# One core, attention and two mixtures of experts: a third expert taken in pairs of quarters, the last row tiles in ascending order, one group of relus behind a minimum

## The chip, the cores and the metric

The kernel runs on one core of a Trainium2 chip. A time is the device time in microseconds (us) of one execution. Five engines work side by side, each through its own list of instructions in order: TensorE (PE; its weight loads are shown as PEld), VectorE (DVE), ScalarE (ACT), GpSimd (POOL) and SyncE (SP), which issues most DMAs. They wait for one another by semaphores.

## The reference, cut to what matters

```python
def _attn_ref(q, k, v, w1, b1, w2):                  # 2 x 8 heads, 576 positions, 64 per head
    scores = scale * np.matmul(q, k.transpose(0, 1, 3, 2))
    x = (log1p(|i - j|) / log1p(max(i, 1)))[..., None]
    bias = np.maximum(x @ w1 + b1, 0.0) @ w2          # 32 hidden, 8 heads
    scores = scores + bias.transpose(2, 0, 1)[None]
    attn = softmax(scores)
    return np.matmul(attn, v)

def _moe_ref(x, w_gate, w1, w2, capacity):            # 1152 tokens, 8 experts, at most 288 each
    expert_idx = np.argmax(x @ w_gate, axis=1)
    ...
    h = np.maximum(np.einsum('ecd,edf->ecf', disp, w1), 0.0)
    y = np.einsum('ecf,efd->ecd', h, w2)              # 512 -> 1024 -> 512
    out[i] = gate_w[i] * y[expert_idx[i], pos[i]]     # a token over capacity stays zero

def _moe2_ref(x, w_in, w_out, alpha):                 # 512 -> 2048 -> 512, dense
    h = x @ w_in
    return (np.maximum(h, 0.0) + alpha * np.minimum(h, 0.0)) @ w_out
```

The dense layer's weights come in 64 bits and are turned into 32 bits on the chip. The matmuls of the experts and of the dense layer take each operand as two parts, a rounded high one and the rest (names that end in h and l), and add three products.

## The kernel before, in words

The program has five stages.

- Head: tables of relus make the position bias. `bias_h` computes four relu tiles of a block of 16 query rows (`h`, most on DVE at L183), `bias_mm` multiplies them (L192), `bias_out` scales the result on ACT (L200) and writes it to a scratch tensor `bd`, from where `load_bias` and `load_bias4` read it back as `bias`.
- Course: units of attention in slots. In a slot PE computes the scores of one unit, DVE adds the bias and takes the row minimum of the negated scores (`low`, L266), ACT takes the exponential (`expo`, L273), and PE turns the result of an earlier unit and multiplies it by the values. The first slots also carry what is left of the bias blocks: `tiles(1)` issues the four relus of one block, `blocks(2)` the matmuls of two. The order of PE, ACT and DVE in this stage is the order of the code.
- The first expert (`job`): 288 rows, eight steps; a step has 12 matmuls of `layer1` (L690) and 12 of `layer2` (L705). Quarters of the weights are split by `raw_split` into high and low parts, on ACT (L602) and DVE (L603).
- The second and the third expert, beside each other (`two_groups`). The second runs as `job` does. The third has at most 32 rows and goes along as a `rider`: its steps are called from inside the second expert's eight, at the numbers in the table `RT` (step 2f stands after `layer1` of f, 2f+1 after `layer2` of f-1). A rider transposes its rows, then takes four quarters of the weights: `partial` (four matmuls, side by side in four groups of 32 columns of the array), a copy on ACT (L803), `hidden` (fold, two matmuls, a relu on ACT), and later `layer2`; `load2` fetches the second weights into the room of the first. `ahead` converts the first weights of the dense layer in steps 3, 5 and 7.
- The dense layer (`ffn`): 608 rows in five tiles of 128 (the last has 96), 16 steps of 24 matmuls of `layer1` (L941) and 15 of `layer2` (L953). At its end each row tile gets the last two steps' six matmuls, is scaled by the gate on ACT (L979) or DVE (L981), and POOL scatters it to `out` (L982).

In the last two stages the code is not the order: a scheduler with a model of the costs places the instructions of every engine, and they then run in that order. It also keeps two engines from one tile, so that a matmul into a tile of two banks waits until the scale of the other half has been read. `facc` is such a tile: row tiles 0 and 1 share one, 2 and 3 another, and row tile 4 has `facc4` to itself.

## Time and profile before

| what | value |
|---|---|
| median of 3 runs | 359.77 us (359.17 to 360.88) |
| the profiled execution | 359.0 us, span 357.3 us |
| head and course | about 0 to 171 us of the span |
| second expert with the rider | 203 to 239 us |
| dense layer, to its last matmul | 239 to 350 us |
| last scatters and the end | 350 to 357 us |

The span runs from the first to the last instruction. The profile gives the busy time of each engine, the instructions in order of time with the idle time ahead of each and what ended it, the waits summed by pair, and the DMAs with the time from issue to landing. A 32-bit matmul stands in it as two records, so that four of them are "x8".

### The profile page before, as it was taken

How to read it: one execution, taken by the hardware profiler on the slowest of the kernel's cores; microseconds unless marked ns; L12 is line 12 of the kernel's file. 1: busy time of each engine (PE TensorE's matmuls, PEld its weight loads, DVE VectorE, ACT ScalarE, POOL GpSimd, SP SyncE). 2: the span in 40 equal slices, each digit the busy share in tenths (PEclk: the TensorE clock that was granted, in tenths of full speed). 3: DMA queues.
4: the chain of work that ended last, by engine and by line, in shares of the span. 5: the costliest groups of instructions: out<-in, count | busy, mean ns of one | idle time of the engine just before them, and what ended most of it. 6: DMA issues, size and time to landing. Idle time of an engine off the chain costs nothing. (4 is left out here: it accounts for less than half of the span.)

```text
span 357.3 us, 8970 instructions
## 1 busy us (share of the span) xinstructions
PE 339.5 (95%) x3372; PEld 273.2 (76%) x3373; DVE 278.7 (78%) x674; ACT 236.4 (66%) x585; POOL 58.8 (16%) x90
## 2 busy tenths in 40 slices
PE   4898999999999999999999999999999999999991
PEld 2334566677899788888899997799988988987880
DVE  4999989977788867876798795369999999988430
ACT  6959899987667675766774473357776656656430
POOL 2055333300000010462262100100000000000023
PEclk9999999999999999999999999999999999999997
DMA  7788969898999853948736996743546645530003
GB/s 301 223 257 273 333 244 354 313 285 313 339 411 337 276 206 108 332 154 258 222 71 189 361 288 187 246 150 125 178 119 189 190 152 178 175 120 3 0 29 118
DMA packets 42048, 76.90 MB, mean 215 GB/s; under 512 B 5159, under 2 KB 19623, under 8 KB 41996
## 3 DMA queue, kind: packets, MB, share of 16 engines
q1 hardware_dynamic: 40812, 73.76, 63.0%
q0 software_dynamic: 1184, 2.48, 1.9%
q8 instruction: 28, 0.46, 0.6%
q14 instruction: 24, 0.20, 0.2%
HBM read 57.53 MB, written 20.09 MB: 217 GB/s over the span
## 5 line engine op out<-in xcount | busy, mean ns | idle before, releaser
L273 ACT ACTIVATE p<-p,mn 128x576 f32<-128x576 f32 x72 | 55.6, 779 | 11.4 <-DVE mn L266 11.2
L259 PE MATMUL sps<-kqv 64*128 64x288 f32 x256 | 61.3, 427 | 0.3 <-DVE mn L266 0.2
L266 DVE CUSTOM_DVE_ANT_0 p<-sps,bias 128x576 f32<-128x576 f32 x72 | 52.4, 751 | 6.2 <-PE sps L252 3.6
L305 PE MATMUL t<-ident,p 64*128 64x64 f32 x640 | 52.6, 227 | 0.6 <-DVE PT L282 0.2
L183 DVE TENSOR_SCALAR h<-c 128x512 f32<-128x512 f32 (+17 forms) x121 | 49.5, 474 | 0.5 <-PE bps L192 0.4
L305 PEld LDWEIGHTS t<-ident,p 64*128 64x128 f32 x640 | 45.3, 139 | 6.0 <-ACT st L200 2.6
L280 ACT COPY PT<-t 128x320 f32<-128x320 f32 (+1 forms) x85 | 30.0, 404 | 24.7 <-PE sps L259 18.6
L259 PEld LDWEIGHTS sps<-kqv 64*128 64x128 f32 x256 | 37.2, 187 | 8.0 <-issue 4.1
L192 PE MATMUL bps<-h,c 128*32 128x512 f32 (+17 forms) x352 | 34.4, 489 | 8.0 <-DVE h L183 5.3
L323 PE MATMUL av<-PT,kqv 128*64 128x128 f32 x512 | 35.3, 279 | 0.8 <-ACT PT L280 0.3
L323 PEld LDWEIGHTS av<-PT,kqv 128*64 128x64 f32 x512 | 27.5, 137 | 8.6 <-ACT PT L280 4.1
L860 ACT ACTIVATE cv<-d 128x512 f32<-128x512 f32 x32 | 21.6, 676 | 14.8 <-DMA d<-in_win 5.5
L200 ACT ACTIVATE st<-bps,c 128x527 f32<-128x527 f32 (+35 forms) x72 | 30.6, 506 | 0.2 <-PE bps L192 0.2
L953 PE MATMUL facc<-w2h,hl 128*128 128x512 f32 (+1 forms) x75 | 29.9, 399 | 0.2 <-DVE hl L603 0.2
L953 PE MATMUL facc<-w2h,hh 128*128 128x512 f32 (+1 forms) x75 | 29.7, 396 | 0.0
L953 PE MATMUL facc<-w2l,hh 128*128 128x512 f32 (+1 forms) x75 | 29.6, 395 | 0.0
L192 PEld LDWEIGHTS bps<-h,c 128*32 128x32 f32 x352 | 10.6, 113 | 23.8 <-issue 7.4
L179 POOL TENSOR_SCALAR h<-c 128x448 f32<-128x448 f32 (+11 forms) x12 | 21.6, 1798 | 36.2 <-PE bps L192 19.5
L941 PE MATMUL fg<-yh,w1l 128*128 128x304 f32 x120 | 26.6, 303 | 0.0
L941 PE MATMUL fg<-yl,w1h 128*128 128x304 f32 x120 | 26.5, 302 | 0.0
L941 PE MATMUL fg<-yh,w1h 128*128 128x304 f32 x120 | 26.5, 302 | 0.0
L282 DVE COPY PT<-t 128x320 f32<-128x320 f32 (+1 forms) x43 | 18.8, 461 | 9.0 <-PE t L305 8.0
(232 smaller groups left out, 691.2 us busy)
## 6 DMA issues: line engine op xcount, KB each, us to landing
bias<-bd SPq DMA_DIRECT2D x23, 576.0 KB, 6.8
bd<-st SPq DMA_DIRECT2D x36, 295.5 KB, 6.7
raw<-in_ew SPq DMA_DIRECT2D x20, 512.0 KB, 6.5
d<-in_win SPq DMA_DIRECT2D x16, 512.0 KB, 3.8
d<-in_wout SPq DMA_DIRECT2D x16, 512.0 KB, 3.9
kqv<-in_kqva SPq DMA_DIRECT2D x6, 736.0 KB, 7.0
kqv<-in_kqvb SPq DMA_DIRECT2D x6, 672.0 KB, 9.3
xd<-zr SPq DMA_DIRECT2D x4, 722.8 KB, 8.6
```

The source lines that it names most:

```text
L179: G.tensor_scalar(h, tab[:, :n], psi[:, i:i + 1], 0.0, ALU.add, ALU.max)
L183: V.tensor_scalar(h, tab[:, :n], psi[:, i:i + 1], 0.0, ALU.add, ALU.max)
L192: T.matmul(ps[32 * c:32 * c + 32, n0:n1], w2n, hs[c][:, n0:n1], start=True, stop=True)
L200: A.activation(st[:, o:o + src.shape[1]], src, AF.Copy, scale=rr[:, t:t + 1])
L259: return [lambda n=n: T.matmul(ps[:, n, :288], q[u.ul][p], k[p, 288 * n:288 * n + 288], start=True, stop=True) for n in range(2)]
L266: V.tensor_tensor_reduce(out.rearrange("p (a b) -> p a b", a=2), ps[:, :, :288], bias.rearrange("p (a b) -> p a b", a=2), -0.125, 3.0e38, ...
L273: A.activation(out, out, AF.Exp, bias=mn, scale=-1.0, accum_out=acc)
L280: A.copy(o, i)
L305: return [lambda i=i, x=x: T.transpose(src[:, i], x[p], ident[p, p]) for i, x in enumerate(rows)], out
L323: T.matmul(o[p, c], u.v[:, j, p], rhs(h, j), start=j == 0, stop=False, skip_group_check=True)
L941: T.matmul(ps, w[:, 128 * k:128 * k + 128], x[:, k, s], start=k + i == 0, stop=k + i == 5)
L953: T.matmul(acc[i][:m], h[:, r:r + m], w, start=f == 0 and j == 0, stop=f == NF - 1 and j == 2)
```

## The change

Three edits. The rider takes two quarters in a call: `partial` puts two quarters into one tile of accumulators and copies 512 columns at once, `hidden` folds four pieces and takes one relu, `layer2` runs two quarters; the calls come at other steps, and so does `load2`. The last row tiles go in the order 0, 1, 2, 3, 4 in the code, 0 and 2 on DVE, 1 and 3 on ACT, and 4 in two halves, one on each. In slot 1 of the course the relus of one block are issued after the slot's minimum.

```diff
--- before.py
+++ after.py
@@ -33,7 +33,7 @@
 BIG = float(1 << 20)
 PRE0 = 10
 NB = 2
-RT = (0, 1, 2, 3, 4, 5, 6, 7, 9, 11, 12)
+RT = (4, 5, 7, 8, 10, 12, 14)
 Q3 = 1
 PRE = 4
 
@@ -794,29 +794,30 @@
                     T.transpose(ps[:, k], xr[:, 128 * k:128 * k + 128], ident[:n, :n])
                 V.tensor_copy(x, ps)
 
-            def partial(q):
-                w = S[q]
-                ps = ps1(pt, "part")[:, 0:256]
-                for k in range(4):
-                    T.matmul(ps[n * k:n * k + n], x[:, k], w[k], start=True, stop=True, skip_group_check=True)
-                R.p = cell()[:, 0:256]
+            def partial(*qs):
+                ps = ps1(pt, "part")
+                for q in qs:
+                    for k in range(4):
+                        T.matmul(ps[n * k:n * k + n, 256 * (q % 2):256 * (q % 2) + 256], x[:, k], S[q][k], start=True, stop=True,
+                                 skip_group_check=True)
+                R.p = cell()
                 A.copy(R.p, ps)
 
-            def hidden(q):
-                ps = ps1(pt, "hT")[:, 0:2 * n]
-                for j in range(2):
+            def hidden(*qs):
+                ps = ps1(pt, "hT")[:, 0:4 * n]
+                for j in range(4):
                     T.matmul(ps[:, n * j:n * j + n], R.p[:, 128 * j:128 * j + 128], fold[:, 2 * n:3 * n], start=True, stop=True)
-                A.activation(R.h[:, 2 * n * q:2 * n * q + 2 * n], ps, AF.Relu)
-
-            def layer2(q):
-                if q == 0:
+                A.activation(R.h[:, 2 * n * qs[0]:2 * n * qs[0] + 4 * n], ps, AF.Relu)
+
+            def layer2(*qs):
+                if 0 in qs:
                     R.acc = ps1(pt, "racc")[:, 0:256]
-                w = S[q]
-                for j in range(2):
-                    for d in range(2):
-                        o = n * (2 * j + d)
-                        T.matmul(R.acc[o:o + n], R.h[:, n * (2 * q + j):][:, 0:n], w[j][:, 256 * d:256 * d + 256],
-                                 start=q == 0, stop=q == 3, skip_group_check=True)
+                for q in qs:
+                    for j in range(2):
+                        for d in range(2):
+                            o = n * (2 * j + d)
+                            T.matmul(R.acc[o:o + n], R.h[:, n * (2 * q + j):][:, 0:n], S[q][j][:, 256 * d:256 * d + 256],
+                                     start=q == 0, stop=q == 3, skip_group_check=True)
 
             def finish():
                 y = cell()[:, 0:256]
@@ -831,10 +832,9 @@
                 V.tensor_tensor(yl, ps, yh.bitcast(F32), ALU.subtract)
 
             return begin, [(i, lambda f=f, q=q: f(*q)) for i, f, *q in (
-                (RT[0], transpose), (RT[1], partial, 0), (RT[1], load2, 0),
-                (RT[2], hidden, 0), (RT[2], partial, 1), (RT[2], load2, 1), (RT[3], hidden, 1), (RT[3], partial, 2), (RT[3], load2, 2),
-                (RT[4], hidden, 2), (RT[4], partial, 3), (RT[4], load2, 3), (RT[5], hidden, 3), (RT[6], layer2, 0),
-                (RT[7], layer2, 1), (RT[8], layer2, 2), (RT[9], layer2, 3), (RT[10], finish))]
+                (RT[0], transpose), (RT[1], partial, 0, 1), (RT[1], load2, 0), (RT[1], load2, 1),
+                (RT[2], hidden, 0, 1), (RT[2], partial, 2, 3), (RT[2], load2, 2), (RT[2], load2, 3), (RT[3], hidden, 2, 3),
+                (RT[4], layer2, 0, 1), (RT[5], layer2, 2, 3), (RT[6], finish))]
 
         def to_dense(acc, yo, n):
             for d in range(2):
@@ -968,13 +968,13 @@
                     prev = h
 
             ys = [z.bitcast(F32).rearrange("p (i n) -> p i n", i=2) for z in M.d]
-            for i in [i for i in (0, 2, 1, 3, 4) if i < len(rows)]:
+            for i in range(len(rows)):
                 r, m = rows[i]
                 layer2(i, NF - 2, *prev)
                 layer2(i, NF - 1, *h)
                 gt, ti = gts[i]
                 y = ys[i // 2][:, i % 2]
-                c = 0 if i in (2, 3) else DM
+                c = DM // 2 if i == 4 else DM if i % 2 else 0
                 if c > 0:
                     A.activation(y[:m, 0:c], acc[i][:m, 0:c], AF.Copy, scale=gt[:m, 0:1])
                 if c < DM:
@@ -1123,8 +1123,6 @@
                                   "places", "gates r2", "s0", "r3", "s1", "r4 s2", "s3", "s4 second", "", "halves", ""):
                             late.append([dict(first=first_weights, second=second, halves=first_halves).get(x) or st[x]
                                          for x in z.split()])
-                if i == 1:
-                    tiles(1)
                 turns(t, u)
                 expo(u)
                 b = blocks(2)
@@ -1138,7 +1136,7 @@
                     tiles(1)
                 if w:
                     b()
-                if nh < NT and i != 1:
+                if nh < NT:
                     tiles(1)
                 if u.short:
                     mix(scores(u.short, 0))
```

What moves on the engines. First, DVE in slot 1; `h` are relu tiles, `p,mn<-sps,bias` is the minimum of slot 1:

```order
 L183 TENSOR_SCALAR h<-c_81 128x448 x3
 L183 TENSOR_SCALAR h<-c_81 128x432 x4
+L266 ISA p_417,mn<-sps,bias_277 128x576
+L266 ISA mn 128x1
 L183 TENSOR_SCALAR h<-c_81 128x416 x3
-L266 ISA p_425,mn<-sps,bias_277 128x576
-L266 ISA mn 128x1
 L183 TENSOR_SCALAR h<-c_81 128x400 x4
```

The minimum moves ahead of three relus of one block.

Second, PE beside the second expert's step 4, from a fold of the rider on (`hT`; `part` is `partial`, `g` and `acc` are the second expert's own). Before:

```order
L808 MATMUL hT<-fold,cell 128x32 x2
L690 MATMUL g_3852<-xh,w1h 128x288
L690 MATMUL g_3852<-xl,w1h 128x288 x2
L801 MATMUL part<-raw_3393,m 32x256 x4
L690 MATMUL g_3852<-xl,w1h 128x288 x2
L690 MATMUL g_3852<-xh,w1l 128x288 x2
L808 MATMUL hT<-fold,cell 128x32 x2
L801 MATMUL part<-xj,m 32x256 x4
L690 MATMUL g_3852<-xh,w1l 128x288 x2
L705 MATMUL acc<-hh,w2h 128x288 x2
L808 MATMUL hT<-fold,cell 128x32 x2
L705 MATMUL acc<-hh,w2h 128x288 x2
```

And now:

```order
L809 MATMUL hT<-fold,cell 128x32 x4
L801 MATMUL part<-raw_3393,m 32x256 x4
L690 MATMUL g_3827<-xl,w1h 128x288 x2
L690 MATMUL g_3827<-xh,w1l 128x288
L801 MATMUL part<-xj,m 32x256 x2
L690 MATMUL g_3827<-xh,w1l 128x288 x2
L801 MATMUL part<-xj,m 32x256 x2
L690 MATMUL g_3827<-xh,w1l 128x288
L705 MATMUL acc<-hh,w2h 128x288 x4
L705 MATMUL acc<-hh,w2l 128x288
L809 MATMUL hT<-fold,cell 128x32 x4
L705 MATMUL acc<-hh,w2l 128x288 x3
```

The fold has four matmuls instead of two, and the last quarter's `partial` (`part<-xj`) stands in two pieces of two with the second expert's matmuls between them, where it stood in one. In the same stage, DVE behind the split of the first quarter (`w1l_...<-raw` is the split of the second quarter's first weights, `cv`, `cw` and `ah` belong to `ahead`). Before:

```order
L694 SCALAR_TENSOR_TENSOR hl_3662<-g1_3648,hh_3661 128x288 [waits Activation_49]
L862 TENSOR_SCALAR ah1_3437<-cv_3794 128x512 [waits Activation_49]
L863 SCALAR_TENSOR_TENSOR ah1_3437<-cv_3794,ah1_3437 128x512 [waits DVE_49]
L603 TENSOR_TENSOR w1l_3673<-raw_3630,w1h_3672 128x1024 [waits DMAHW7_49,Activation_49]
L694 SCALAR_TENSOR_TENSOR hl_3702<-g1_3688,hh_3701 128x288 [waits Activation_49]
L864 SCALAR_TENSOR_TENSOR ah1_3437<-d2_3119,ah1_3437 128x512 [waits DMAHW6_49,DVE_49]
```

And now:

```order
L694 SCALAR_TENSOR_TENSOR hl_3662<-g1_3648,hh_3661 128x288 [waits Activation_49]
L862 TENSOR_SCALAR cw_3702<-cv_3703 128x512
L862 TENSOR_SCALAR ah1_3437<-cv_3749 128x512 [waits Activation_49]
L863 SCALAR_TENSOR_TENSOR cw_3702<-cv_3703,cw_3702 128x512 [waits DVE_49]
L603 TENSOR_TENSOR w1l_3666<-raw_3630,w1h_3665 128x1024 [waits DMAHW7_49,Activation_49]
L694 SCALAR_TENSOR_TENSOR hl_3687<-g1_3673,hh_3686 128x288 [waits Activation_49]
```

A further conversion (`cw_3702<-cv_3703`, L862) stands ahead of the split of `w1l`, and its second step (L863) has taken the place of the other conversion's.

Third, the end of the dense layer on PE, the last 12 matmuls. Before (`facc_4028` holds row tiles 2 and 3):

```order
L953 MATMUL facc_4028<-w2h_4881,hh_5037 128x512 [waits DVE_49]
L953 MATMUL facc_4028<-w2l_4882,hh_5037 128x512
L953 MATMUL facc_4028<-w2h_4881,hl_5038 128x512
L953 MATMUL facc_4028<-w2h_4881,hh_5090 128x512
L953 MATMUL facc_4028<-w2l_4882,hh_5090 128x512
L953 MATMUL facc_4028<-w2h_4881,hl_5091 128x512
L953 MATMUL facc4_4029<-w2h_4881,hh_5037 96x512
L953 MATMUL facc4_4029<-w2l_4882,hh_5037 96x512
L953 MATMUL facc4_4029<-w2h_4881,hl_5038 96x512
L953 MATMUL facc4_4029<-w2h_4881,hh_5090 96x512
L953 MATMUL facc4_4029<-w2l_4882,hh_5090 96x512
L953 MATMUL facc4_4029<-w2h_4881,hl_5091 96x512
```

And now (`facc_4018` holds row tiles 2 and 3):

```order
L953 MATMUL facc4_4019<-w2h_4871,hh_5027 96x512
L953 MATMUL facc4_4019<-w2l_4872,hh_5027 96x512
L953 MATMUL facc4_4019<-w2h_4871,hl_5028 96x512
L953 MATMUL facc4_4019<-w2h_4871,hh_5080 96x512
L953 MATMUL facc4_4019<-w2l_4872,hh_5080 96x512
L953 MATMUL facc_4018<-w2h_4871,hh_5027 128x512 [waits DVE_49]
L953 MATMUL facc_4018<-w2l_4872,hh_5027 128x512
L953 MATMUL facc_4018<-w2h_4871,hl_5028 128x512
L953 MATMUL facc_4018<-w2h_4871,hh_5080 128x512
L953 MATMUL facc_4018<-w2l_4872,hh_5080 128x512
L953 MATMUL facc_4018<-w2h_4871,hl_5081 128x512
L953 MATMUL facc4_4019<-w2h_4871,hl_5081 96x512
```

Row tile 3 stood ahead of all six matmuls of row tile 4; now five of row tile 4's six stand ahead of it, and its six wait for DVE's scale of row tile 2. DVE at the same place, before:

```order
L603 TENSOR_TENSOR hl_5091<-g_3123,hh_5090 128x304 [waits PE_49,Activation_49]
L945 SCALAR_TENSOR_TENSOR g_3123<-m_3122,malpha_108,g_3123 128x304 [waits Activation_49]
L603 TENSOR_TENSOR hl_5091<-g_3123,hh_5090 128x304 [waits Activation_49]
L981 TENSOR_SCALAR d1_3118<-facc_4028,gt_4015 128x512 [waits PE_49]
L981 TENSOR_SCALAR d1_3118<-facc_4028,gt_4019 128x512 [waits PE_49]
```

And now:

```order
L945 SCALAR_TENSOR_TENSOR g_3123<-m_3122,malpha_108,g_3123 128x304 [waits Activation_49]
L981 TENSOR_SCALAR d0_3117<-facc_4017,gt_3997 128x512 [waits PE_49]
L603 TENSOR_TENSOR hl_5081<-g_3123,hh_5080 128x304 [waits Activation_49]
L981 TENSOR_SCALAR d1_3118<-facc_4018,gt_4005 128x512 [waits PE_49]
L981 TENSOR_SCALAR d2_3119<-facc4_4019,gt_4013 96x256 [waits Activation_49]
```

DVE now scales row tile 0 ahead of the last split `hl`, and its half of row tile 4 waits for ACT, whose half is ahead.

## Rows read from the trace of the kernel before

**Rows 1.** The page, part 1: busy us (share of the span) xinstructions.

```profile
PE 339.5 (95%) x3372; PEld 273.2 (76%) x3373; DVE 278.7 (78%) x674; ACT 236.4 (66%) x585; POOL 58.8 (16%) x90
```

**Rows 2.** Busy us by engine in two stretches, then clock, DMA share, GB/s.

```profile
220.00:240.00 20.00, 20.00 (x158) 16.41 (x158) 9.10 (x15) 8.80 (x19) 1.19 (x5) 1.00 0.62 192
240.00:260.00 20.00, 20.00 (x123) 18.45 (x122) 19.68 (x40) 14.22 (x33) 0.00 (x0) 1.00 0.48 154
```

**Rows 3.** Timeline of DVE, 20 to 38: start, us, line, out<-in, xcount [idle before <-releaser].

```profile
21.74 4.35 DVE L183 TENSOR_SCALAR h<-c 128x448 f32<-128x448 f32 x10
26.02 0.74 DVE L266 CUSTOM_DVE_ANT_0 p<-sps,bias 128x576 f32<-128x576 f32 x1
28.66 0.76 DVE L266 CUSTOM_DVE_ANT_0 p<-sps,bias 128x576 f32<-128x576 f32 x1 [0.53 <-DMA bias<-bd]
...
36.61 0.76 DVE L266 CUSTOM_DVE_ANT_0 p<-sps,bias 128x576 f32<-128x576 f32 x1 [0.35 <-DMA bias<-bd]
```

**Rows 4.** Timeline of the DMA queue, the last load of the second bias.

```profile
20.95 0.59 SPq L164 DMA_DIRECT2D bias<-bd  x1
```

**Rows 5.** DMA issues at that time: KB each, us from issue to landing.

```profile
bias<-bd SPq DMA_DIRECT2D x1, 16.0 KB, 4.4
```

**Rows 6.** Timeline of ACT, the second slot.

```profile
26.80 0.78 ACT L273 ACTIVATE p<-p,mn 128x576 f32<-128x576 f32 x1 [2.49 <-DVE mn L266]
```

**Rows 7.** Timeline of PE, the rider's blocks (a 32-bit matmul is two records).

```profile
214.16 0.64 PE L801 MATMUL part<-ah,m 128*32 128x256 f32 x8
214.73 0.79 PE L705 MATMUL acc<-hh,w2l 128*128 128x288 f32 x4
215.36 0.57 PE L808 MATMUL hT<-fold,cell 128*128 128x32 f32 x4
215.76 0.51 PE L705 MATMUL acc<-hl,w2h 128*128 128x288 f32 x2
...
219.74 0.61 PE L808 MATMUL hT<-fold,cell 128*128 128x32 f32 x4
220.28 0.64 PE L801 MATMUL part<-xj,m 128*32 128x256 f32 x8
220.85 0.40 PE L690 MATMUL g<-xh,w1l 128*128 128x288 f32 x1
...
230.92 0.63 PE L818 MATMUL racc<-xj,cell 128*32 128x256 f32 x4
231.48 0.40 PE L690 MATMUL g<-xh,w1l 128*128 128x288 f32 x1
```

**Rows 8.** Timeline of DVE ahead of the second quarter's split.

```profile
206.85 0.42 DVE L862 TENSOR_SCALAR ah<-cv 128x512 int32<-128x512 int32 x1
207.91 1.22 DVE L603 TENSOR_TENSOR w1l<-raw,w1h 128x1024 fp32r<-128x1024 f32 x1
```

**Rows 9.** Timeline of PE, where it needs that split.

```profile
209.19 0.79 PE L690 MATMUL g<-xh,w1l 128*128 128x288 f32 x4
```

**Rows 10.** Lines by form, ACT, 214 to 222: busy, mean ns | idle before.

```profile
L803 ACT COPY cell<-part 128x256 f32<-128x256 f32 x4 | 1.5, 372 | 3.0 <-PE part L801 3.0
```

**Rows 11.** Timeline of PE, its last two matmuls.

```profile
348.94 0.40 PE L953 MATMUL facc<-w2l,hh 128*96 128x512 f32 x1
349.17 0.39 PE L953 MATMUL facc<-w2h,hl 128*96 128x512 f32 x1
```

**Rows 12.** Timeline of DVE, scale of row tile 3.

```profile
348.22 0.75 DVE L981 TENSOR_SCALAR d<-facc,gt 128x512 f32<-128x512 f32 x1 [2.02 <-PE facc L953]
```

**Rows 13.** Timeline of ACT, scale of row tile 4.

```profile
349.60 0.68 ACT L979 ACTIVATE d<-facc,gt 96x512 f32<-96x512 f32 x1 [2.08 <-PE facc L953]
```

**Rows 14.** Timeline of POOL, the last two scatters.

```profile
349.74 0.97 POOL L982 DMA_INDIRECT out<-d,ti  x1 [0.49 <-issue]
351.09 0.93 POOL L982 DMA_INDIRECT out<-d,ti  x1 [0.38 <-POOLq L1284]
```

**Rows 15.** Who waited, PE weight loads, 310 to 330: us, times, longest.

```profile
PEld facc L953 <- DVE hl L603: 1.0, 2, 0.7
```

## The prediction

> **What bounds the kernel.** I read the page's busy shares first, then the busy time of single stretches, then the order of time on DVE, PE and ACT at the three places that the edits touch, and last the end of the program. In the page PE is busy 95% of the span [rows 1], and where the second expert and the dense layer run it is busy 20.00 of 20 us at a clock of 1.00 [rows 2]. A PE that is always busy hides what comes late on others, and has no idle time to give back: there a change pays by fewer or cheaper matmuls, and costs by dearer ones or by a stall. Two places differ. At the beginning the slots are set by a chain from bias to minimum to exponential: ACT idles 2.49 us ahead of the second slot's exponential, for DVE's minimum [rows 6]. At the end PE starts its last matmul at 349.17 [rows 11], and what follows is one chain: scale, scatter, landing, to 357.3.
>
> **Slot 1 (the relus).** DVE runs ten relus from 21.74 for 4.35 us, 0.435 each, and the minimum starts at 26.02 [rows 3]. With three relus behind it, DVE would come to it about 1.3 us earlier, at 24.72. But the minimum also needs its bias: the last load of it is issued at 20.95 [rows 4] and takes 4.4 us to land [rows 5], so 25.35. The minimum starts at about 25.5 and the exponential, now at 26.80, at about 26.3: 0.5 earlier. That gain meets the next gates. The minimum of slot 2 waits for the DMA of its bias until 28.66, and a later one until 36.61 [rows 3]. Neither the issue of these loads nor the blocks ahead of them is moved by the edit. The three relus, moved behind the minimum, are still done ahead of the next block's use: seven relus and a minimum from 25.5 take 3.8 us, to 29.3 at worst if all seven are ahead of slot 2's minimum, 0.6 later than now; but then four of those seven stood there before too, and DVE had 0.53 to spare [rows 3], so 0.1 or nothing. Bounds: 0.5 faster, if the gain gets past the gates, and 0.3 slower, if DVE's 0.6 of new idle time isn't made up. I take 0.1 faster, since two gates in the trace are transfers.
>
> **The rider in pairs.** The number of matmuls is the same, so the price lies in how often PE changes over to the rider. From the start of a block to the start of the matmul behind it, a `partial` of four takes 214.16 to 214.73, 0.57; a fold of two 215.36 to 215.76, 0.40; a fold with a `partial` directly behind it 219.74 to 220.85, 1.11; a block of only two second-layer matmuls 230.92 to 231.48, 0.56 [rows 7]. So two matmuls cost as much as four: most of it is the changeover. The order of PE before has three `partial` blocks, three folds and one joined pair: 3 x 0.57 + 3 x 0.40 + 1.11 = 4.02. Now there are two quarters in blocks of their own, one quarter behind a fold of four, and one quarter in two pieces: 4 x 0.57 = 2.28 with the pieces at 0.57 each, a joined fold at 1.11 + 0.40 = 1.51, and a fold of four, 0.80. That is 4.59, so 0.55 slower. The pairing saves two folds and gives them twice as many matmuls, and the scheduler cuts one quarter in two. Bounds: if a fold of four costs the 0.40 of two, 4.59 - 0.80 = 3.79, 0.2 faster; if joining gives nothing, 0.6 slower. The second layer's `racc` stands in five blocks before and after, so nothing there.
>
> Two more terms come with the new steps. On DVE a second conversion of 0.42 [rows 8] now stands ahead of the split of the second quarter's first weights. That split starts at 207.91 and takes 1.22 [rows 8], to 209.13, and PE starts the matmuls that read it at 209.19 [rows 9], so there is no slack: 0.4 slower. It costs nothing if the scheduler's earlier work on DVE ends sooner than now, and 0.4 is the most. DVE was 9.10 busy of 20 us a little later [rows 2], so the delay ends there. On ACT the copy of the accumulators is 512 wide instead of 256, of which four took 372 ns each, with 3.0 us of waiting for `partial` ahead of them [rows 10]; by the scale of 512 columns, 0.68 [rows 13], it takes 0.3 longer. The folds stand behind other matmuls of PE, which hide most of it: 0.1, bounds 0 and 0.3. `load2` comes at other steps, and so on the queue of SP the last raw quarter stands ahead of it. The room for it comes free when a quarter's `partial` pair is done, and the second layer is eight steps behind: I cost it at nothing; if a load were late, PE would stall by what is left of its some 4.4 us [rows 5]. The sum for the rider is 0.55 + 0.4 + 0.1 = 1.05 slower.
>
> **The end.** Before, row tile 3 is complete ahead of the six matmuls of row tile 4. DVE scales it from 348.22, 0.75 [rows 12], and POOL scatters it from 349.74, 0.97, while PE still works [rows 14]. The scale of row tile 4 starts at 349.60, 0.68 [rows 13], which is 0.43 behind the start of the last matmul, and the last scatter starts at 351.09 [rows 14], 0.81 behind the end of that scale. In the new order of PE five of row tile 4's matmuls stand ahead of row tile 3's six, since these wait until DVE has scaled row tile 2 in the other half of the same tile. The next to last matmul completes row tile 3: 348.94 [rows 11] + 0.43 = 349.37, which is 1.15 later than 348.22. On ACT 0.68: 350.05. From the end of that scale before (348.22 + 0.75) to its scatter (349.74) are 0.77: 350.82. The last scatter follows the one before by 351.09 - 349.74 = 1.35: 352.17, against 351.09. Row tile 4's halves don't set this: ACT's half is about as long as the 256-wide copy, 0.37 [rows 10], and ends at 350.42, DVE's, which waits for it, about 0.45 later at 350.87; with 0.8 to the scatter, 351.67, 0.5 ahead of POOL. So 1.1 slower, with no other engine to hide it. Bounds: 0.15 faster, if row tile 3 is no later and only the last scale shortens; 1.4 slower, if row tile 3's matmuls also wait for the scale of row tile 2 (0.75, of which the five matmuls of row tile 4 at 0.23 cover most).
>
> The order of DVE shows its half waiting for ACT: the halves don't overlap, and two halves one behind the other take 0.8 where one scale took 0.68. The Trainium skill's "PSUM — Partial Sum Buffer", section "PSUM bank collisions raise a hardware error", forbids two engines in the same bank and quadrant at once, even for two reads. By that rule a tile's halves can never run side by side, so this part of the edit would gain nothing even with row tile 3 back in its place: the tail would come out 0.1 to 0.2 slower, where without the rule the shorter scale gives 0.15. No run of the kernel before shows two engines on one bank.
>
> **The sum.** -0.1 + 1.05 + 1.1 = 2.05 slower. The profiled execution took 359.0, so 361.0 by itself; the median of the three runs, 359.77, lies 0.8 above it. I forecast the median: 359.77 + 2.05 = 361.8.
>
> **The rivals.**
> (a) Faster or the same, by one mechanism: the price of a rider's block is a wait for a fresh tile of accumulators, not the change in shape. Then a pair pays it once, at the first block: two `partial` calls and two folds, 2 x 0.57 + 2 x 0.40 = 1.94, 2.1 less than 4.02. With the other terms (0.5 and 1.1, less 0.1) 359.2. It decides as soon as the rider saves 1.5. For it: two matmuls cost as much as four. Against it: the block at 230.92 goes on in a tile already begun, and still pays 0.56 [rows 7].
> (b) The end is harmless: the last row tile decides alone, and the earlier scatters hide behind it. Then -0.1 + 1.05 is left: 360.7. Against it: POOL's two last scatters are 1.35 apart [rows 14], so a late row tile 3 delays both.
> (c) The rider's delay is taken up later: the dense layer waits for DVE between 310 and 330, twice, 1.0 us in all [rows 15], and DVE is 19.68 of 20 us busy when it begins [rows 2]. If DVE goes on there while PE is late, PE's delay is paid out of that wait: 359.77 - 0.1 + 1.1 = 360.8. Against it: most of DVE's work in the dense layer is released by PE's own matmuls.
> (d) The front's 0.5 gets past the gates: 361.4.
> (e) The reverse of (c): the dense layer's DVE is pushed back with PE by other conversions, and that wait doubles, 1.0 more: 362.8.
>
> **Chances.** Half a per cent, 1.8 us, is about what a measurement can tell from no change: faster ends at 357.97, slower begins at 361.57. The forecast has 0.40, its own range 361.0 to 362.5, and 0.28 of it lies above 361.57. (a) 0.13: 0.06 faster, if the end is harmless too, otherwise the same. (b) 0.15, 0.02 of it slower. (c) 0.15, 0.03 of it slower. (d) 0.05, 0.02 slower. (e) 0.12, slower. Together slower 0.47, faster 0.06, the same 0.47. The range for 8 in 10 goes from 359.4, just above (a), to 363.0, just above (e); with the bounds of the terms it leaves out about 0.1 on each side.
>
> **What would show it.** Slot 1's minimum at about 25.5, behind a wait for its DMA, and slot 2's still at about 28.7 and the later one at 36.6: a shift of 0.5 kept after 36.6 makes (d) right. The rider's `partial`, fold and `racc` blocks, start to the next start: if four fold matmuls take 0.40 or the second piece of the cut quarter costs little, (a). The split of the second quarter's first weights ending near 209.5, with a gap of PE behind it: without a gap 0.4 goes. The dense layer beginning about 1.0 later against the end of the first expert. The wait of 1.0 between 310 and 330: gone with (c), doubled with (e). Row tile 3's scale on ACT only some 0.2 ahead of the completion of row tile 4, DVE's half behind ACT's, and the last scatter 3.0 instead of 1.9 behind the start of PE's last matmul: if it stays 1.9, (b). The forecast as a whole is wrong if the dense layer begins no later than before, or if the end is no longer.

## The result

The changed kernel took 363.53 us (median of 6 runs, 362.48 to 365.71), the kernel before 359.72 (6 runs, 359.17 to 360.88): a ratio of 1.010, 95% interval 1.0058 to 1.0142. That is 3.8 us slower, above the range of the forecast (359.4 to 363.0, likeliest 361.8), and later experiments repeat only 1.1 of it. The profiled execution is the fastest of the six: 362.48, span 360.7, against 359.0 and 357.3.

Both programs fall into the same stages, so the 3.5 us between the spans can be laid out by stage. The marks are the first minimum of slot 0, the first `layer1` matmul of the first expert, the first matmul of the dense layer, PE's last matmul, the start of the last scatter, and the end.

| stage, us | before | changed | difference |
|---|---|---|---|
| to the first minimum (same program) | 21.06 | 22.00 | +0.94 |
| first minimum to the first expert | 153.20 | 155.67 | +2.47 |
| both experts, with the rider | 64.59 | 65.27 | +0.68 |
| dense layer, to the last matmul | 110.32 | 109.45 | -0.87 |
| last matmul to the last scatter | 1.91 | 2.93 | +1.02 |
| last scatter to the end | 6.17 | 5.41 | -0.76 |

The first two terms, 3.4 in all, lie ahead of the experts, where the forecast had 0.1 faster. The first of them is chance: over all seventeen profiles, those of the experiments below included, the first minimum starts at 20.85 to 22.79 with either program. The page shows a busy PE as before [rows 1]:

```profile
PE 340.0 (94%) x3372; PEld 274.5 (76%) x3373; DVE 277.3 (77%) x675; ACT 235.9 (65%) x581; POOL 58.4 (16%) x90
```

**Slot 1.** DVE's order of time in the changed kernel, to be read against [rows 3]:

```profile
22.00 0.76 DVE L266 CUSTOM_DVE_ANT_0 p<-sps,bias 128x576 f32<-128x576 f32 x1 [0.69 <-DMA bias<-bd]
22.68 3.07 DVE L183 TENSOR_SCALAR h<-c 128x448 f32<-128x448 f32 x7
...
26.60 0.76 DVE L266 CUSTOM_DVE_ANT_0 p<-sps,bias 128x576 f32<-128x576 f32 x1 [0.84 <-PE bps L192]
27.28 2.84 DVE L183 TENSOR_SCALAR h<-c 128x416 f32<-128x416 f32 x7
30.04 0.74 DVE L266 CUSTOM_DVE_ANT_0 p<-sps,bias 128x576 f32<-128x576 f32 x1
...
37.05 0.76 DVE L266 CUSTOM_DVE_ANT_0 p<-sps,bias 128x576 f32<-128x576 f32 x1
```

From the first minimum to slot 1's are 4.60 us (4.96 before), with 0.84 of idle time ahead of it. Then seven relus stand ahead of slot 2's, which comes 8.04 behind the first (7.60 before), without idle time: 0.4 later, where the forecast said 0.1 or nothing. At the last row shown it is 15.05 against 15.55, but over seven profiles with the edit (14.77 to 15.53) and ten without (15.06 to 15.55) the mean is 15.1 and 15.2. No gain or loss is left that stands out of this spread.

**The stall.** The 2.5 us are in one place, the interval between two minima near 157 (6.24 us, before 3.74). Both times DVE stands ahead of the same copy, of the attention weights times the values (`av`) out of the accumulators. PE's last matmuls for it and the copy, first before, then changed:

```profile
154.12 0.29 PE L325 MATMUL av<-pt,vd 128*64 128x64 f32 x4
154.45 0.42 DVE L327 COPY xT<-av 128x128 f32<-128x128 f32 x2 [1.03 <-PE av L325]
```

```profile
155.11 0.29 PE L325 MATMUL av<-pt,vd 128*64 128x64 f32 x4
157.71 0.42 DVE L327 COPY xT<-av 128x128 f32<-128x128 f32 x2 [3.29 <-PE sps L259]
```

PE's last matmul for that copy starts at 154.18 before and 155.18 in the changed kernel; the copy follows 0.27 behind it in the one and 2.53 in the other. It is not DVE that is late. The copy waits for PE's semaphore alone, and the trace has the changes of that semaphore: at 154.43 before and at 157.68 in the changed kernel, both times 0.02 ahead of the copy. So PE's signal came late; between 153.24 and 157.68 the changed kernel's trace has no change of it at all. Neither the order of the code nor a wait of this place is touched by the change.

**The rider.** PE, start to next start [rows 7]:

```profile
217.79 0.64 PE L801 MATMUL part<-ah,m 128*32 128x256 f32 x8
218.36 0.79 PE L705 MATMUL acc<-hh,w2l 128*128 128x288 f32 x4
...
219.60 0.64 PE L801 MATMUL part<-raw,m 128*32 128x256 f32 x8
220.17 0.81 PE L690 MATMUL g<-xh,w1h 128*128 128x288 f32 x4
...
221.08 0.97 PE L809 MATMUL hT<-fold,cell 128*128 128x32 f32 x8
221.98 0.64 PE L801 MATMUL part<-raw,m 128*32 128x256 f32 x8
222.55 0.54 PE L690 MATMUL g<-xl,w1h 128*128 128x288 f32 x2
...
223.15 0.62 PE L801 MATMUL part<-xj,m 128*32 128x256 f32 x4
223.71 0.53 PE L690 MATMUL g<-xh,w1l 128*128 128x288 f32 x2
224.17 0.62 PE L801 MATMUL part<-xj,m 128*32 128x256 f32 x4
224.72 0.40 PE L690 MATMUL g<-xh,w1l 128*128 128x288 f32 x1
...
225.63 0.97 PE L809 MATMUL hT<-fold,cell 128*128 128x32 f32 x8
226.44 0.65 PE L705 MATMUL acc<-hh,w2l 128*128 128x288 f32 x3
```

The blocks take 0.57, 0.57, 0.90 + 0.57, 0.56, 0.55 and 0.81: 4.53 in all. A piece of two matmuls costs what a whole quarter costs, and a fold of four twice a fold of two. Two folds of before that [rows 7] leave out, 0.43 and 0.47:

```profile
217.53 0.59 PE L808 MATMUL hT<-fold,cell 128*128 128x32 f32 x4
217.96 0.38 PE L690 MATMUL g<-xh,w1h 128*128 128x288 f32 x1
...
221.49 0.63 PE L808 MATMUL hT<-fold,cell 128*128 128x32 f32 x4
221.96 0.51 PE L705 MATMUL acc<-hh,w2h 128*128 128x288 f32 x2
```

The split of the second quarter's first weights [rows 8] stands behind two conversions, and PE waits for it [rows 9]:

```profile
210.28 0.42 DVE L862 TENSOR_SCALAR cw<-cv 128x512 int32<-128x512 int32 x1
210.61 0.42 DVE L862 TENSOR_SCALAR ah<-cv 128x512 int32<-128x512 int32 x1
210.94 0.68 DVE L863 SCALAR_TENSOR_TENSOR cw<-cv,cw 128x512 int32<-128x512 int32 x1
211.55 1.22 DVE L603 TENSOR_TENSOR w1l<-raw,w1h 128x1024 fp32r<-128x1024 f32 x1
```

```profile
212.04 0.68 PE L690 MATMUL g<-xl,w1h 128*128 128x288 f32 x4
212.82 0.79 PE L690 MATMUL g<-xh,w1l 128*128 128x288 f32 x4
```

PE's step to the next four is 0.78 us, where it was 0.58 (208.61 to 209.19): 0.2 of stall, not 0.4. The first conversion is no longer followed by the one that reads it, and takes 0.33 to the next start. Before, it was followed by that one, 0.45 behind its start at 206.85 [rows 8]:

```profile
207.30 0.69 DVE L863 SCALAR_TENSOR_TENSOR ah<-cv,ah 128x512 int32<-128x512 int32 x1
```

**The end** [rows 11 to 14]. ACT, DVE and POOL in the changed kernel, whose last matmul starts at 352.39:

```profile
352.59 1.05 ACT L979 ACTIVATE d<-facc,gt 128x512 f32<-128x512 f32 x2 [2.08 <-PE facc L953]
```

```profile
353.67 0.48 DVE L981 TENSOR_SCALAR d<-facc,gt 96x256 f32<-96x256 f32 x1 [2.87 <-ACT d L979]
```

```profile
354.04 0.97 POOL L982 DMA_INDIRECT out<-d,ti  x1 [0.51 <-issue]
355.32 0.93 POOL L982 DMA_INDIRECT out<-d,ti  x1 [0.30 <-issue]
```

Row tile 3's scale starts 0.20 behind the start of the last matmul, its scatter 1.65 and the last scatter 2.93, as worked out (0.20, 1.65, 3.0). ACT's row holds two instructions, the scale of row tile 3 and ACT's half of row tile 4; DVE's half follows it.

**The dense layer.** PE's wait for `hl` [rows 15], 1.0 before, is gone but for 0.2:

```profile
PEld facc L953 <- DVE hl L603: 0.2, 1, 0.2
```

### The profile page after: what moved, and what is told of

Same layout as the page of the kernel before. It is cut to its first block, busy times and chain, and to the rows that moved or that the text cites. A ratio compares the mean times of both kernels' runs of the same rounds, so it can differ in the third digit from the quotient of the medians.

```text
span 360.7 us, 8973 instructions
## 1 busy us (share of the span) xinstructions
PE 340.0 (94%) x3372; PEld 274.5 (76%) x3373; DVE 277.3 (77%) x675; ACT 235.9 (65%) x581; POOL 58.4 (16%) x90
## 4 chain that ended last, share of the span: by engine, by line
PE 79%; DVE 7%; DMA 6%; ACT 3%; issue 2%; SPq 2%; POOL 1%; POOLq 0%; DVEq 0%; ACTq 0%
PE facc L953 15%; PE fg L941 15%; PE av L323 9%; PE sps L259 7%; PE t L305 7%; PE acc L705 7%; PE g L690 6%; PE bps L192 4%; DVE h L183 3%; DMA kqv<-in_kqva 2%; PE av L325 2%; DMA bias<-bd 1%; DMA bd<-st 1%; DMA c<-in_c 1%; DVE p L266 1%
## 5 line engine op out<-in xcount | busy, mean ns | idle before, releaser
L259 PE MATMUL sps<-kqv 64*128 64x288 f32 x256 | 60.1, 426 | 0.5 <-DMA kqv<-in_kqva 0.5
L183 DVE TENSOR_SCALAR h<-c 128x512 f32<-128x512 f32 (+17 forms) x121 | 48.7, 467 | 0.9 <-PE bps L192 0.8
L192 PE MATMUL bps<-h,c 128*32 128x512 f32 (+17 forms) x352 | 35.2, 503 | 7.8 <-DVE h L183 5.8
L192 PEld LDWEIGHTS bps<-h,c 128*32 128x32 f32 x352 | 11.4, 115 | 23.7 <-issue 8.1
```

The source lines that it names most:

```text
L183: V.tensor_scalar(h, tab[:, :n], psi[:, i:i + 1], 0.0, ALU.add, ALU.max)
L192: T.matmul(ps[32 * c:32 * c + 32, n0:n1], w2n, hs[c][:, n0:n1], start=True, stop=True)
L259: return [lambda n=n: T.matmul(ps[:, n, :288], q[u.ul][p], k[p, 288 * n:288 * n + 288], start=True, stop=True) for n in range(2)]
```

## The experiments

Each was timed in five rounds beside the kernel before on the same chip, in four jobs on three chips; which chip the first comparison ran on is not on record. Ratios are to the kernel before, with 95% intervals, and are not always those of the medians: an interval of 0.2 to 0.3% either way is some 0.7 to 1.1 us.

### First job: each edit alone, and the changed kernel again

The edit of slot 1 alone:

```
-                if i == 1:
-                    tiles(1)
                 turns(t, u)
...
-                if nh < NT and i != 1:
+                if nh < NT:
                     tiles(1)
```

> Only the edit of slot 1 (three relus of one block behind the minimum). In the changed kernel's profile the first expert begins 3.4 us later than before: 1.0 of it is there by slot 20, 2.5 come in one stall of DVE and PE near 157. Theory 1, the stall and the late beginning are chance of one execution: this kernel is within 0.5 us of before, its first expert begins within 1 us of before. Theory 2, the edit itself costs the course: 2 to 3.5 us slower, with the first expert that much later, in the median of all rounds. Theory 3 (the forecast's bounds): between 0.5 faster and 0.3 slower.

358.49 against 357.96 us, ratio 1.0011 (0.9984 to 1.0039). From the first minimum to the first expert 151.87, less than in any profile shown so far. Theory 2 falls on this chip and theory 1 fits; the interval, from 0.6 faster to 1.4 slower, is too wide to hold the forecast's bounds against it.

The pairs alone: `partial(*qs)`, `hidden(*qs)`, `layer2(*qs)`, `RT = (4, 5, 7, 8, 10, 12, 14)` and the list of steps as in the change, the rest as before.

> Only the rider in pairs. The forecast has 1.05 slower, all of it between the start of the second expert and the start of the dense layer. The changed kernel's profile shows 0.7 between these and 0.9 given back inside the dense layer. Theory 1, the dense layer takes the delay up: 0 to 0.3 slower in all. Theory 2, what it gives back is chance: 0.7 to 1.1 slower. Theory 3, the pairs cost the front too, by the code that stands behind it: over 1.5 slower.

358.36, ratio 1.0001 (0.9981 to 1.0022). The experts take 65.27 (before 64.59), the dense layer 109.46. Theory 1 fits: the rider's 0.7 is there, and the dense layer is 0.5 shorter than in the profile above (109.98). The time alone doesn't show it, since the interval reaches 0.8 slower.

The end alone:

```
-            for i in [i for i in (0, 2, 1, 3, 4) if i < len(rows)]:
+            for i in range(len(rows)):
...
-                c = 0 if i in (2, 3) else DM
+                c = DM // 2 if i == 4 else DM if i % 2 else 0
```

> Only the order of the last row tiles and the halves. The forecast has 1.1 slower, from row tile 3 whose scale comes behind the next to last matmul, with the last scatter 3.0 us behind the start of PE's last matmul instead of 1.9. Rival: the landing of the last scatter takes less when two tiles' scatters stand close together (in the changed kernel's profile the end comes 5.4 us behind the last scatter's start, 6.2 before), so 0.3 slower.

359.35, ratio 1.0027 (1.0003 to 1.0051), so 1.0 slower. The last scatter is 2.93 behind the last matmul. From there to the end it took 5.46, in the two kernels above 5.79 and 5.70, as the rival has it; one profile each is too little to tell it from chance.

The changed kernel, unchanged, for a second profile:

> The changed kernel once more, for a second profile and ten more times. Theory 1 (the stall near 157 is chance of that execution): no stall there, first expert 0 to 1 us later than before, and 1.5 to 2.5 slower in the median. Theory 2 (the change brings it): the stall is there again and the median is 3 to 4 us above before.

359.11, ratio 1.0030 (1.0006 to 1.0054): 1.15 slower. No stall near 157; the interval is 3.74, as before. Experts 65.27, dense layer 109.44, end 2.93.

### Second job: the end taken apart, and the slot edit taken out

> The changed kernel once more, to see what of its time depends on the chip. Stage by stage the last profile had: experts 65.27 us from the first layer1 matmul to the dense layer (before 64.59), dense layer 109.44 (before 110.32, and 109.98 in a kernel whose dense layer is the same), last matmul to last scatter 2.93 (before 1.91). Theory 1: these come back within 0.2, the time from the first minimum to the first expert varies without the edit, and the median is 0.8 to 1.8 us above before. Theory 2: on some chips the change costs the course 2 to 3 us (a stall as at 157 in its first profile), and the median is 3 to 4 us above before.

358.72 against 357.66, ratio 1.0034 (1.0015 to 1.0054). Experts 65.26, dense layer 109.42, end 2.93, no stall. The same chip as in the first job, so it says nothing of other chips.

The changed kernel with slot 1 as before (`if i == 1: tiles(1)` ahead of `turns`):

> The changed kernel with slot 1 as before. Theory 1 (the slot edit does nothing): within 0.5 us of the changed kernel run beside it. Theory 2 (the slot edit brings the stall in the course): 2 to 3 us faster than the changed kernel, if that is slow on this chip. By the forecast's terms 0.1 slower than the changed kernel.

358.76 beside 358.72: no effect of the slot edit that can be told from chance. Ratio 1.0017 (1.0000 to 1.0033), which overlaps with that of the changed kernel.

Only the halves, in the old order:

```
-                c = 0 if i in (2, 3) else DM
+                c = 0 if i in (2, 3) else DM // 2 if i == 4 else DM
```

> The kernel before with row tile 4 scaled in two halves, row tiles in the old order. By the forecast's working row tile 3 is then early again, ACT's half ends at about 0.4 and DVE's, which waits for ACT, about 0.45 later, against 0.68 for one scale: the last scatter 0.1 to 0.2 later, so 2.0 to 2.1 us behind the start of the last matmul (1.91 before). If the halves ran side by side: 1.76. No difference in the time that a measurement can tell.

The last scatter comes 2.22 behind the last matmul, 0.31 later than before, where 0.1 to 0.2 was expected. ACT's half, then DVE's, in this kernel:

```profile
349.89 0.47 ACT L979 ACTIVATE d<-facc,gt 96x256 f32<-96x256 f32 x1 [2.09 <-PE facc L953]
```

```profile
350.39 0.48 DVE L981 TENSOR_SCALAR d<-facc,gt 96x256 f32<-96x256 f32 x1 [1.14 <-ACT d L979]
```

The halves take 0.47 and 0.48, 0.98 from first start to last end, against 0.68 for one scale: half the columns cost two thirds of the time. The Trainium skill's page "PSUM — Partial Sum Buffer", section "PSUM bank collisions raise a hardware error", forbids two engines in one bank and quadrant at once. The trace agrees in so far as DVE's half starts 0.03 behind the end of ACT's; but that order is the scheduler's, and whether the halves could overlap was not tried. In the time: ratio 1.0018 (0.9998 to 1.0038), not clear.

Only the ascending order, row tile 4 in one piece:

```
-            for i in [i for i in (0, 2, 1, 3, 4) if i < len(rows)]:
+            for i in range(len(rows)):
...
-                c = 0 if i in (2, 3) else DM
+                c = DM if i in (1, 3, 4) else 0
```

> The kernel before with the row tiles in ascending order (0 and 2 on DVE, 1, 3 and 4 on ACT), row tile 4 in one piece. If row tile 3's lateness is what the end costs, all of the 1.0 us is here: last scatter 2.9 to 3.0 us behind the start of the last matmul, as in the kernel with the whole edit of the end. If the halves cost it, 1.9 as before.

2.94, so all of the end's 1.0 is the lateness of row tile 3, and beside it the halves are hidden behind POOL. Ratio 1.0011 (0.9992 to 1.0030): not clear of no change, nor of the 1.0 us that the end should cost.

### Third job: what the dense layer waits for

In the kernel before, ACT's conversion of the last block of `w_in` waits for its load, and what hangs on it ends in the wait for `hl` [rows 15]. ACT in the kernel before, then in the kernel with the pairs alone:

```profile
316.39 0.66 ACT L860 ACTIVATE cv<-d 128x512 f32<-128x512 f32 x1 [2.29 <-DMA d<-in_win]
```

```profile
316.50 0.67 ACT L860 ACTIVATE cv<-d 128x512 f32<-128x512 f32 x1 [1.05 <-DMA d<-in_win]
```

From the start of the dense layer (238.85 and 240.15) these are 77.54 and 76.35 us. This conversion sets the length of the dense layer where it is late. In the five profiles where it starts 76.83, 77.20, 77.54, 77.85 and 78.20 us behind the start of the dense layer (the old rider in all), that layer takes 109.58, 109.98, 110.32, 110.62 and 110.97, each 32.75 to 32.78 more. In the ten others without an early load it starts at 75.93 to 76.73, and the layer takes 109.42 to 109.48. All eight profiles with pairs are among these ten. Counted from the first matmul of the first expert the conversion starts at the same time with either rider, 141.7 on average with pairs and 141.8 without: PE comes 0.7 later to a load that is no later.

The edit gives that load a tile of its own and issues it earlier, in the kernel before:

```
+            def room(i):
+                return AH["more"].bitcast(I32) if i == 30 else M.d[i % 3]
             def fetch(i):
-                if i < 2 * NF:
-                    f64_load(i, M.d[i % 3])
+                if i < 2 * NF and i != 30:
+                    f64_load(i, room(i))
+                if i == 27:
+                    f64_load(30, room(30))
...
-                        f64_convert(M.d[(2 * f + w) % 3], src)
+                        f64_convert(room(2 * f + w), src)
```

> The kernel before with one load of the dense layer (the last block of w_in) put into a free tile of its own and issued three loads earlier. In four profiles with the old rider that load lands 76.7 to 78.1 us behind the start of the dense layer, ACT's conversion waits for it, and PE waits 0.6 us or more for hl at 84; the dense layer takes 109.58 to 110.97. In five profiles with the pairs it lands by 76.6 and the dense layer takes 109.42 to 109.46. Theory 1 (the dense layer gives the rider's delay back because the loads are early against PE): with the load early the dense layer takes 109.4 to 109.6 with the old rider too, and the whole is about 0.9 us faster than before. Theory 2 (the pairs' other order of the conversions on DVE does it): 109.6 to 111.0 as before, no gain.

356.70 against 357.19, ratio 0.9991 (0.9976 to 1.0007); dense layer 109.47.

> The kernel before, unchanged, as a measure of chance. Time within 0.4 us of the runs of the kernel before beside it; dense layer 109.6 to 111.0 us, experts 64.6, last matmul to last scatter 1.91.

357.56, ratio 1.0015 (0.9998 to 1.0033): a kernel against itself moves by 0.4 us. In this execution the load lands 76.50 behind the start of the dense layer, and the dense layer takes 109.48 without any early load. The expectation of 109.6 or more was too narrow, and so the early load shows no gain that can be told from chance.

> The changed kernel once more. Theory 1 (what was over 1.1 us in the first comparison belongs to those executions): 0.8 to 1.8 us above before. Theory 2 (the change costs the course 2 to 3 us on some chips): 3 to 4 us above before.

358.48, ratio 1.0034 (1.0017 to 1.0050): 1.3 slower by the medians on a second chip, no stall.

### Fourth job: a third chip

> The changed kernel once more. Theory 1 (the excess over 1.2 us belongs to the executions of the first comparison): 0.8 to 1.8 us above before. Theory 2 (some chips): 3 to 4 us above before if this is such a chip, with the loss ahead of the first expert.

361.74 against 360.62, ratio 1.0025 (1.0003 to 1.0048).

> Only the slot edit, on the same chip as the changed kernel. Theory 1: within 0.5 us of before. Theory 2: 2 to 3 us slower where the changed kernel is 3 to 4 slower.

359.55, ratio 1.0000 (0.9968 to 1.0031): no difference shown.

> The changed kernel without the slot edit. Theory 1: within 0.5 us of the changed kernel, 0.6 to 1.4 above before. Theory 2: 2 to 3 us faster than the changed kernel where that is 3 to 4 slower than before.

361.39, ratio 1.0024 (1.0005 to 1.0043).

> The kernel before with the last load of w_in issued three loads earlier, for a narrower interval. If PE's wait at 84 us into the dense layer costs before 0.7 us on average (six profiles of the old rider: 109.48 to 110.97, mean 110.16, floor 109.45), 0.5 to 0.9 us faster than before; dense layer 109.4 to 109.6.

360.60, ratio 1.0004 (0.9986 to 1.0022); dense layer 109.50. No gain, so no version here beats the kernel before.

On this chip all four profiles have the stall. The kernel before was timed here but not profiled; it takes longer too (358.3 to 363.1, median 360.62, against 357.2 to 358.0 on the two other chips), and the changed kernel is only 1.1 above it. The copy near 157 in the changed kernel, in the one without the slot edit, and in the kernel before with the early load; the last two have the course of the kernel before:

```profile
156.11 0.42 DVE L327 COPY xT<-av 128x128 f32<-128x128 f32 x2 [3.14 <-PE sps L259]
```

```profile
156.68 0.42 DVE L327 COPY xT<-av 128x128 f32<-128x128 f32 x2 [4.15 <-PE t L305]
```

```profile
155.31 0.42 DVE L327 COPY xT<-av 128x128 f32<-128x128 f32 x2 [2.82 <-PE sps L259]
```

The interval between the two minima is 6.08, 6.65 and 6.44 us there, 6.45 with the slot edit alone, and 3.74 in all eleven profiles of the first three jobs. In each the change of PE's semaphore stands 0.02 ahead of the copy, as above. So theory 2 falls: the stall is there with the course edited and unedited, and the changed kernel's profile is without it three times.

Three of these four, the changed kernel, the one without the slot edit and the early load, have a second loss right behind the stall. From 160.1, 158.9 and 158.5 on the clock granted to PE is at the lower of its two levels, 1.2 GHz, for 3.4 us, after PE had stood idle for part of the stall (in the last, PE was busy 0.77 of the two microseconds from 156 to 158). Elsewhere every profile has that level only behind PE's last matmul, in the last 3 to 6 us of the span. Their first expert starts 155.98 to 156.63 behind the first minimum; in the fourth, where the clock stays up, 154.53. In the changed kernel's twelve executions on this chip the mean of the granted clock (1 is the higher level) goes with the time: 362.23 to 363.08 us for the five at 0.988 to 0.991, 359.41 to 361.85 for the seven at 0.993 to 0.995.

## Why the prediction was wrong

**The step that failed is the last one, "359.77 + 2.05".** It carried the time of before's runs over to the changed kernel's, as if the stages that the change doesn't touch took the same time in both: it put them at nothing, without a reason. They don't. From the profiled runs: 362.48 - 359.0 = 3.48, of which the interval near 157 holds 6.24 - 3.74 = 2.50. Of the 0.98 that is left 0.94 is the later first minimum, chance as well, so that the edits as good as cancel out in this one pair of profiles; that 0.98 comes near the 0.9 to 1.2 of the four later comparisons (1.0025 to 1.0034) is luck. The range had bounds for every edit and none for an untouched stage.

What the rows show in its place is PE's signal for one copy, 2.3 us later behind PE's matmul than before (157.68 - 155.18 against 154.43 - 154.18), at the higher clock and with DVE idle. Why it was in the changed kernel's profile and not in before's stays open; so does what held PE's signal. The changed kernel's other five runs, which have no profile here, had a mean granted clock of 0.985 to 0.990 of full speed, lower than every profile here (0.991 to 0.996). On the third chip such runs are the longer ones, which suggests the stall and the lower clock behind it in these five too, but doesn't show it.

**And the sum of 2.05 was itself too high.** Stage by stage:

- Slot 1, -0.1: right in mechanism, nothing in size. Slot 1's minimum came 0.5 earlier against the first minimum on average (4.5 for 5.0 us). The next gates took it, though by DVE's seven relus (slot 2's minimum 0.4 later, without idle time), not by a DMA. With and without the edit the time is the same within the noise (358.72 and 358.76), so rival (d) falls too.
- The rider, +1.05: 0.65 to 0.69 in all eight profiles of pairs. The blocks cost 4.53 against 4.12 before, measured the same way (four `partial` at 0.57, folds at 0.40, 0.43, 0.54 and 0.47): 0.41 for the forecast's 0.55 (by its own terms, 4.59 - 4.02, 0.57). The conversion cost 0.2 for 0.4: in these rows the one that depends on the other starts 0.45 behind it, the one that doesn't 0.33. What is left, 0.04 to 0.08, is within the wide copy's 0.1, which no row shows by itself.
- Rival (a) falls: the experts got longer, not 1.5 or more shorter, and the racc blocks and the cut pieces pay 0.55 and more for two matmuls within one tile. The rider's `part` and `racc` rows have the form 128*32 and their neighbours 128*128; the Trainium skill's "TensorEngine Tiling (Array Packing)", section "Key Properties", says that a change of tiling mode drains the engine, and the 0.55 to 0.57 of a block, whether of two matmuls or of four, agrees; no run here tells a drain from another price of the change. The folds have the form 128*128, and pay per matmul (0.40 for two, 0.81 for four).
- Rival (c) is what happened. With pairs the dense layer took 109.42 to 109.46 in eight profiles; with the old rider 109.47 to 110.97 in seven (mean 110.06), longer one for one with the conversion of the last load of `w_in` where that starts 76.83 us or more behind the layer's start. Rival (e), the reverse, falls with it. The forecast gave this 0.15, on the ground that PE's matmuls release DVE's work; here a load did. The early load doesn't prove it, since on both of its chips the wait was gone from a profile without it too, and the time of the pairs alone (ratio 1.0001, interval to 1.0022) is too rough to. The profiles side by side show it: PE 0.68 late to a conversion that is no later. By the same rows nothing is given back in an execution whose load is early, as in two of the seven with the old rider.
- The end, +1.1: 1.02 to the start of the last scatter in every profile, all from row tile 3's place, so rival (b) falls. Some 0.3 of it may come back behind that: from the start of the last scatter to the end are 5.57 us on average in eight profiles with the edit (5.34 to 5.95), 5.84 in seven without (5.51 to 6.17). These ranges overlap, so this is not shown. The forecast had no term for it.

Together, with averages over executions for the third and the last term: 0 + 0.68 - 0.62 + 1.02 - 0.27 = 0.8, against 0.9 to 1.2 measured in the later comparisons. Of the forecast's cases (c), 1.0 slower, comes nearest.

## What to carry to other kernels

Where PE is the bound, count the places at which it changes to a differently shaped matmul, and not the matmuls alone: grouping calls saved nothing here, since the scheduler cut a group again. A delay ahead of a stage that waits for loads may be taken out of that wait; look for the last DMA behind the stage's stalls before adding the delay to the sum. And a forecast of a time on another execution needs a term for the stages that nobody touches: compare stage by stage, and time the kernel before beside it on the same chip.

## What the runs showed of the hardware that was not expected

- In a stretch whose order is fixed, PE's signal for one copy came late, and an interval of 3.74 us between two minima grew by 2.3 to 2.9: on one chip in all four profiles, in none of the eleven on two others, and in one of the two of the first comparison. The copy started 0.02 us behind the signal each time.
- In three of the four, the clock granted to PE was at 1.2 GHz for 3.4 us right behind that stall, in which PE had been idle in part.
- Where the dense layer's last load of `w_in` was converted late, 76.83 to 78.20 us into the layer, the layer ended 32.75 to 32.78 us behind the start of that conversion, five times out of five.
- Half the columns of a scale out of the accumulators (96x256) took 0.47 us on ACT and 0.48 on DVE, where all of them took 0.68 (ACT, 96x512) and 0.75 (DVE, 128x512).
- Two conversions on DVE that don't depend on each other start 0.33 us apart, two of which the second reads the first 0.45.
- Eleven timings of the kernel before differ from 27 others of it on the same chip, taken beside them, by 0.4 us in the median.
